# Hourglass attention and an ELU feed-forward on one core: attention rebuilt with four tokens per partition and DMA transposes

## The chip, the core and the metric

The kernel runs on one core of a Trainium2 chip. Its engines are TensorE (PE, matrix products from SBUF into PSUM), VectorE (DVE), ScalarE (ACT), GpSimd (POOL) and SyncE (SP, which here only issues transfers); 16 DMA engines serve them. The metric is the time of one execution on the device, in microseconds (us), on the slowest core; here there is one.

## What is computed

The inputs are q, k and v of shape (8 batches, 8 heads, 576 tokens, 64), float32, and the feed-forward's weights of 512 x 2048 and 2048 x 512. Two attentions are added, and the sum goes through the feed-forward:

```python
# per batch and head; sm_attn = softmax(scale * q k^T) v, softmax with the row maximum subtracted
out_up = np.repeat(sm_attn(mean4(q), mean4(k), mean4(v)), 4, axis=2)   # 144 pooled tokens
mask = np.abs(pos[:, None] - pos[None, :]) < 4                         # 7 neighbours
out_local = softmax(np.where(mask, scale * q @ k.T, -1e9)) @ v
x = (out_up + out_local)            # to 4608 tokens x 512
h = x @ w_in
out = np.where(h > 0, h, np.exp(np.minimum(h, 0)) - 1) @ w_out
```

`mean4` is the mean over four consecutive tokens. The feed-forward takes by far most of the arithmetic.

## The kernel before

Work is cut by batch b and by pair of heads j (four pairs of two heads; a pair fills the 128 partitions with 2 x 64 dimensions). `attn_p1(b, j, den)` loads q, k and v of a pair (rows of 256 bytes, issued by SP), turns q and k by float32 transposes on TensorE (L145, L148) into `qt` and `kt`, sums four tokens on GpSimd (L155, L158), and computes the scores with **keys on partitions** and queries along the free axis: 6 windows of 102 keys by 96 queries (L195) and two halves of the pooled attention (L177). ACT takes the exp without a row maximum (L183, L201); DVE multiplies the local scores by a mask of zeros and ones (L205). The denominators of all 8 heads of a batch, three rows a head, are gathered in one PSUM tile `den` by matmuls with indicator columns (L209, L215).

After the four pairs, `p1_group` takes the reciprocals of `den` (L313) and stores them to DRAM. `attn_p2` reads them back, broadcast over 128 partitions (`rcpb`, L227), multiplies the exps (L233), and multiplies by v (L238, L252); DVE adds the pooled part, each column repeated four times, into `XT` (L257), which holds all 4608 tokens.

The feed-forward runs in nine blocks of 512 tokens. `moe_mm1` makes 16 chunks of 128 hidden units (four matmuls each, L269), then exp on ACT (L274) and two operations on DVE (L276, L277) into `gt`, one buffer. `moe_mm2` makes four output tiles of 16 matmuls each (L287), copied by ACT and stored by SP. The program interleaves them: batch b's `p1` with block b-2's `mm1`, and `p2` of batch b-1 with the same block's `mm2`; three blocks run alone at the end. The weights are loaded on ACT's queue after batch 0's first part and cast by DVE. The framework's planner puts the instructions of each engine into a fixed order from this program order and places the waits; each engine and each queue then runs strictly in order.

## Time and profile before

Three runs: 543.38 us median (539.27 to 544.61). The profiled execution:

| | |
|---|---|
| span, first to last instruction | 543.6 us |
| PE busy | 471.4 us (87%) |
| DVE busy | 283.3 us (52%) |
| ACT busy | 240.5 us (44%) |
| POOL busy | 89.0 us (16%) |
| bytes moved by DMA | 59.53 MB, mean 110 GB/s |
| packets | 136219, of them 120240 under 512 bytes |
| mean granted TensorE clock | 0.953 of full speed |

An engine's busy time is the time in which it executed at least one instruction. A row of a group names the line, the engine, the operation, the tiles written and read, the shapes and the count, then the busy time in us and the mean of one in ns, then the idle time before it and what ended it. Matmuls overlap in the pipeline, so their mean is longer than what each adds to PE's time.

### The profile page before, as it was taken

How to read it: one execution, taken by the hardware profiler on the slowest of the kernel's cores; microseconds unless marked ns; L12 is line 12 of the kernel's file. 1: busy time of each engine (PE TensorE's matmuls, PEld its weight loads, DVE VectorE, ACT ScalarE, POOL GpSimd, SP SyncE). 2: the span in 40 equal slices, each digit the busy share in tenths (PEclk: the TensorE clock that was granted, in tenths of full speed). 3: DMA queues.
4: the chain of work that ended last, by engine and by line, in shares of the span. 5: the costliest groups of instructions: out<-in, count | busy, mean ns of one | idle time of the engine just before them, and what ended most of it. 6: DMA issues, size and time to landing. Idle time of an engine off the chain costs nothing.

```text
span 543.6 us, 8740 instructions
## 1 busy us (share of the span) xinstructions
PE 471.4 (87%) x2952; PEld 251.6 (46%) x2952; DVE 283.3 (52%) x627; ACT 240.5 (44%) x501; POOL 89.0 (16%) x260
## 2 busy tenths in 40 slices
PE   1538588788899998999999999999999877999997
PEld 0325355444444554545454545554545443444443
DVE  1212415733653665477456745774567677728180
ACT  1325463355533663367236723772367102535351
POOL 1113432212122122211122112211210000000000
PEclk9999999987898899989899989998989995999999
DMA  7776755534265435552464246524610340020202
GB/s 232 203 201 199 206 120 143 127 78 123 54 152 133 128 88 134 164 118 60 112 158 122 63 110 159 130 59 109 158 55 1 85 135 24 0 78 0 78 0 77
DMA packets 136219, 59.53 MB, mean 110 GB/s; under 512 B 120240, under 2 KB 129008, under 8 KB 135664
## 3 DMA queue, kind: packets, MB, share of 16 engines
q1 hardware_dynamic: 133488, 50.60, 37.4%
q10 hardware_dynamic: 2688, 8.39, 4.4%
q8 instruction: 23, 0.38, 0.3%
q14 instruction: 20, 0.16, 0.1%
HBM read 49.41 MB, written 9.55 MB: 108 GB/s over the span
## 4 chain that ended last, share of the span: by engine, by line
PE 70%; DMA 11%; DVE 6%; ACT 5%; SPq 4%; issue 2%; POOL 2%; ACTq 0%; POOLq 0%
PE hp L269 24%; PE op L287 24%; PE tp L145 6%; DMA kn<-in_k_dram 4%; PE den L209 3%; PE av L252 3%; PE sc L195 3%; ACT kt L149 2%; DMA w_491<-in_moe_w_out_dram 1%; DMA v_292<-in_v_dram 1%; PE vdp L165 1%; DMA rcpb<-rgd 1%; ACT qt L149 1%; PE davp L238 1%; PE den L215 1%
## 5 line engine op out<-in xcount | busy, mean ns | idle before, releaser
L287 PE MATMUL op<-WO,gt 128*128 128x512 f16 x576 | 132.3, 390 | 0.4 <-DVE gt L277 0.3
L274 ACT ACTIVATE e<-hp 128x512 f16<-128x512 f32 x144 | 85.9, 599 | 79.7 <-PE hp L269 78.1
L277 DVE SCALAR_TENSOR_TENSOR gt<-hp,ec 128x512 f16<-128x512 f32 x144 | 97.2, 686 | 3.2
L287 PEld LDWEIGHTS <-gt 128*128 128x128 f16 x576 | 57.6, 101 | 70.2 <-issue 7.6
L269 PEld LDWEIGHTS <-WI 128*128 128x128 f16 x576 | 55.4, 102 | 66.7 <-issue 10.3
L276 DVE TENSOR_SCALAR ec<-e 128x512 f16<-128x512 f16 x144 | 40.3, 287 | 59.6 <-ACT e L274 59.4
L292 ACT COPY os<-op 128x512 f32<-128x512 f32 x36 | 21.1, 585 | 112.4 <-PE op L287 105.2
L269 PE MATMUL hp<-XT_80,WI 128*128 128x512 f16 x144 | 59.1, 410 | 0.4 <-ACT aex L201 0.4
L205 DVE TENSOR_TENSOR mex<-aex,MASK 102x576 f16<-102x576 f16 x64 | 30.4, 478 | 54.5 <-ACT aex L201 52.3
L269 PE MATMUL hp<-XT_81,WI 128*128 128x512 f16 x144 | 57.7, 400 | 0.0
L269 PE MATMUL hp<-XT_83,WI 128*128 128x512 f16 x144 | 57.1, 397 | 0.0
L269 PE MATMUL hp<-XT_82,WI 128*128 128x512 f16 x144 | 57.1, 397 | 0.0
L243 DVE TENSOR_TENSOR outdt<-davp,rcpb 64x144 f16<-64x144 f32 x64 | 19.5, 304 | 59.8 <-PE davp L238 58.3
L145 PE MATMUL tp<-IDT,qn 128*128 128x128 f32 x128 | 33.2, 349 | 14.5 <-DMA qn<-in_q_dram 7.7
L145 PE MATMUL tp<-IDT,kn 128*128 128x128 f32 x128 | 33.9, 346 | 12.9 <-DMA kn<-in_k_dram 6.9
L201 ACT ACTIVATE aex<-sc 102x288 f16<-102x288 f32 x128 | 42.8, 416 | 4.1 <-PE sc L195 3.4
L252 PE MATMUL av<-anr,vw 102*64 102x96 f16 x384 | 35.2, 225 | 10.1 <-DVE anr L233 8.7
L233 DVE TENSOR_TENSOR anr<-mex,rcpb 102x576 f16<-102x576 f16 x64 | 29.3, 469 | 22.4 <-DMA rcpb<-rgd 21.7
L155 POOL TENSOR_TENSOR th<-kt 128x288 f16<-128x288 f16 x32 | 21.4, 670 | 84.6 <-ACT kt L149 84.5
L155 POOL TENSOR_TENSOR th<-qt 128x288 f16<-128x288 f16 x32 | 21.8, 680 | 82.4 <-ACT qt L149 82.4
L209 PE MATMUL den<-mex,INDC 102*24 102x288 f16 x128 | 32.4, 347 | 1.8 <-DVE mex L205 1.6
L252 PEld LDWEIGHTS <-vw 102*64 102x64 f16 x384 | 25.0, 120 | 18.7 <-issue 7.2
(140 smaller groups left out, 490.7 us busy)
## 6 DMA issues: line engine op xcount, KB each, us to landing
rcpb<-rgd SPq DMA_DIRECT2D x64, 180.0 KB
out_dram<-os SPq DMA_DIRECT2D x36, 256.0 KB
qn<-in_q_dram SPq DMA_DIRECT2D x64, 128.0 KB
kn<-in_k_dram SPq DMA_DIRECT2D x64, 128.0 KB
w32i<-in_moe_w_in_dram ACTq DMA_DIRECT2D x4, 1024.0 KB
w_482<-in_moe_w_out_dram ACTq DMA_DIRECT2D x1, 1024.0 KB
qn<-in_q_dram SPq DMA_DIRECT2D x64, 16.0 KB
w_485<-in_moe_w_out_dram ACTq DMA_DIRECT2D x1, 1024.0 KB
```

What stands on the lines that cost most here:

```text
L145: nc.tensor.transpose(tp[:, 128 * c : 128 * c + 128], srcn[:, c, :, :], IDT[:])
L155: nc.gpsimd.tensor_tensor(out=th[:, w_, :], in0=sl[:, 0 : S : 2], in1=sl[:, 1 : S : 2], op=AB.add)
L201: nc.scalar.activation(out=aex[0:KW, g, :], in_=sc[0:KW, 0:HHALF], func=AF.Exp, scale=SCALE)
L205: nc.vector.tensor_tensor(out=mex[0:KW], in0=aex[0:KW], in1=MASK[0:KW], op=AB.mult)
L209: nc.tensor.matmul(den[0:24, 0:HHALF], INDC[0:KW, rr + g, :], mex[0:KW, g, :], start=False, stop=False,)
L233: nc.vector.tensor_tensor(out=anr[0:KW], in0=mexs[hh][0:KW], in1=rcpb[0:KW, 0:S], op=AB.mult)
L252: nc.tensor.matmul(av[r0 : r0 + 64, co : co + QCH], vw[0:KW, c, hh, :], anr[0:KW, g, co : co + QCH], start=True, stop=True,)
L269: nc.tensor.matmul(hp[:, 0:TBLK], WI[:, dc, 128 * fc : 128 * fc + 128], XT[dc][:, t0 : t0 + TBLK], start=(dc == 0), stop=(dc == DMC - 1),)
L274: nc.scalar.activation(out=e[:], in_=hp[:, 0:TBLK], func=AF.Exp)
L276: nc.vector.tensor_scalar(out=ec[:], in0=e[:], scalar1=1.0, scalar2=-1.0, op0=AB.min, op1=AB.add)
L277: nc.vector.scalar_tensor_tensor(out=gt[:, fc, :], in0=hp[:, 0:TBLK], scalar=0.0, op0=AB.max, in1=ec[:], op1=AB.add,)
L287: nc.tensor.matmul(op_[:, 0:DM], gt[:, fc, 128 * t_ : 128 * t_ + 128], WO[:, fc, :], start=(fc == 0), stop=(fc == FCN - 1),)
```

## The change

Attention is written anew; the feed-forward's arithmetic stays as it was.

- **Layout.** Four consecutive tokens share a partition: `load_main` reads 128 of a batch's 144 groups of four for all eight heads in one transfer of 1 MB, in runs of 1 KB, and the 16 groups left over (tails) are loaded for two or four batches together. Batch 0's q and k are loaded by SP; nearly all else, the weights too, by POOL's queue, through three staging buffers.
- **Turning.** q, k and v are cast to fp16 for a whole batch (`cast_qk`), four tokens are summed by adds of contiguous rows (`pool_sum`), and q and k are transposed by the DMA engines (`dma_start_transpose` on SP, L178) instead of TensorE. `fill_q` puts q into token order (`Q2`).
- **Scores** (`a_unit`, one of eight per batch): **queries on partitions**, windows of 104 keys; the mask is added by a matmul of two small factors that puts -60000 into PSUM before the scores are accumulated. DVE takes the row maximum (L262, L267); ACT takes the exp with it as bias, one instruction per window. The exps are transposed by DMA (L289, L293).
- **Products** (`b_local`, `b_down`): v carries a column of ones, so the denominator comes out as a 65th column; `norm` adds 1e-9, takes the reciprocal and multiplies on DVE. The results are transposed by DMA (L343, L345), and POOL adds local and pooled parts into `XT`, now a ring of three blocks.
- **Order.** Batch 0's attention runs alone. Then 288 slots follow, 32 per block (16 of `mm1`, 16 of `mm2`, four matmuls each), and a table `plan` names the slots at which loads, casts and units of later batches stand. `XT` of batch b must be there by slot 32 b. PSUM is eight banks under one name.

The core of the diff; lines that repeat or only rename are left out:

```diff
-            tp = pt("tp", "tp2", 1024)
-            for c in range(4):
-                nc.tensor.transpose(
-                    tp[:, 128 * c : 128 * c + 128], srcn[:, c, :, :], IDT[:]
-                )
-            nc.tensor.transpose(tp[:, 512:576], srcn[0:64, 4, :, :], IDT[0:64, 0:64])
-            nc.scalar.copy(out=dst[:, off : off + S], in_=tp[:, 0:S])
...
-            nc.vector.tensor_tensor(out=mex[0:KW], in0=aex[0:KW], in1=MASK[0:KW], op=AB.mult)
-            mexs.append(mex)
-            rr = 3 * (2 * j + hh)
-            for g in range(2):
-                nc.tensor.matmul(
-                    den[0:24, 0:HHALF], INDC[0:KW, rr + g, :], mex[0:KW, g, :],
-                    start=False, stop=False,
-                )
-            for g in range(2):
-                last = (j, hh, g) == (3, 1, 1)
-                nc.tensor.matmul(
-                    den[0:24, 0:SD], INDC[0:72, rr + 2, :], dexs[hh][0:72, g, :],
-                    start=False, stop=last,
-                )
...
-            rcpb = sb.tile([128, S + SD], FP16, tag="rcpb", bufs=4, name="rcpb")
-            nc.sync.dma_start(
-                out=rcpb[:],
-                in_=bass.AP(tensor=rgd.tensor, offset=rgd.offset + h3 * HHALF,
-                            ap=[[0, 128], [1, S + SD]]),
-            )
-            anr = sb.tile([128, 2, HHALF], FP16, tag="anr", bufs=4, name="anr")
-            nc.vector.tensor_tensor(
-                out=anr[0:KW], in0=mexs[hh][0:KW], in1=rcpb[0:KW, 0:S], op=AB.mult
-            )
...
-                nc.vector.tensor_tensor(
-                    out=xc, in0=av[r0 : r0 + 64, 0:HHALF],
-                    in1=_rep4(outdt[r0 : r0 + 64, 72 * g : 72 * g + 72]), op=AB.add,
-                )
...
+    def load_main(name, b, eng=None):
+        t = staging(name).rearrange("p (h x) -> p h x", h=H)
+        s = srcs[name][b].rearrange("h (a r) d -> a h (r d)", r=4)
+        (eng or nc.gpsimd).dma_start(out=t, in_=s[0:128])
+        stage[name, b] = t
...
+    nat = {}
+
+    def cast_qk(name, b, eng, pool=None):
+        t = stage.pop((name, b))
+        n = sb.tile([128, 5, 512], FP16, tag="nat", bufs=2, name="nat_" + name)
+        cast(qk_view(n), t, 0, 128, SCALE if name == "q" else 1.0, eng)
+        pool_sum(n[:, 4, :], n, 0, 128, 512, pool)
+        nat[name, b] = n
...
+    def turn_qk(name, b):
+        n = nat.pop((name, b))
+        dst = QT if name == "q" else KT
+        nc.sync.dma_start_transpose(
+            out=dst[:].rearrange("p s j a -> p (s j) a")[:, :, 0:128],
+            in_=n[:].rearrange("p s f -> p (s f)"),
+        )
+
+    def fill_k(b, eng):
+        eng.tensor_copy(
+            out=KT[:].rearrange("p s j a -> p (s j) a")[:, :, 128:NQ],
+            in_=KTT[:].rearrange("p s j a -> p (s j) a")[:, :, 16 * b : 16 * b + 16],
+        )
+
+    def fill_q(b, eng, big):
+        eng.tensor_copy(out=QT[:, 4, :, 128:NQ], in_=QTT[:, 4, :, 16 * b : 16 * b + 16])
+        for src, a0, a1, o in ((QTT, 128, NQ, 16 * b - 128), (QT, 0, 128, 0)):
+            big(
+                out=Q2[:, :, 4 * a0 : 4 * a1].rearrange("p j (a r) -> p j r a", r=4),
+                in_=src[:, 0:4, :, a0 + o : a1 + o].rearrange("p r j a -> p j r a"),
+            )
...
+        for c in range(NC6):
+            w = _win(c)
+            n0 = max(0, min(CW, 128 - w))
+            put(0, c, V16, w, n0)
+            if n0 < CW:
+                put(4 * n0, c, V16T, 16 * b, CW - n0)
+        nc.sync.dma_start(out=VDT[0:16, :], in_=VDA[16 * b : 16 * b + 16, :])
...
+    def a_unit(b, j, g):
+        if g == 0:
+            i = serial["a"] % 2
+            serial["a"] += 1
+            cur["P"] = (PL[i], PD[i])
+        pl, pd = cur["P"]
+        bk = [bank("sc"), bank("sc")]
+        for hh in range(2):
+            nc.tensor.matmul(
+                bk[hh][0:NL, 0 : 3 * NK], MU[64 * hh : 64 * hh + 36, :],
+                MV[64 * hh : 64 * hh + 36, g, :], start=True, stop=False,
+                skip_group_check=True,
+            )
+        for cc in range(3):
+            c = 3 * g + cc
+            w = _win(c)
+            for hh in range(2):
+                r0 = 64 * hh
+                nc.tensor.matmul(
+                    bk[hh][0:NL, NK * cc : NK * cc + NK],
+                    Q2[r0 : r0 + 64, j, NL * c : NL * c + NL],
+                    KT[r0 : r0 + 64, 0:4, j, w : w + CW],
+                    start=False, stop=True, skip_group_check=True,
+                )
+        for hh in range(2):
+            r0 = 64 * hh
+            nc.tensor.matmul(
+                bk[hh][0:QH, 3 * NK : 3 * NK + NQ],
+                QT[r0 : r0 + 64, 4, j, QH * g : QH * g + QH],
+                KT[r0 : r0 + 64, 4, j, :], start=True, stop=True,
+                skip_group_check=True,
+            )
+        mx = sb.tile([128, 2, 4], FP32, tag="mx", bufs=4, name="mx")
+        md = sb.tile([128, 2], FP32, tag="md", bufs=4, name="md")
+        for hh in range(2):
+            nc.vector.tensor_reduce(
+                out=mx[0:NL, hh, 0:3],
+                in_=bk[hh][0:NL, 0 : 3 * NK].rearrange("p (c x) -> p c x", c=3),
+                axis=AX.X, op=AB.max, negate=True,
+            )
+            nc.vector.tensor_reduce(
+                out=mx[0:QH, hh, 3:4], in_=bk[hh][0:QH, 3 * NK : 3 * NK + NQ],
+                axis=AX.X, op=AB.max, negate=True,
+            )
+        nc.vector.tensor_scalar(
+            out=md[0:QH, :], in0=mx[0:QH, :, 3], scalar1=0.0625, scalar2=None, op0=AB.mult
+        )
+        for hh in range(2):
+            for cc in range(3):
+                nc.scalar.activation(
+                    out=pl[:, 3 * g + cc, hh, 0:NK].rearrange("p (a r) -> p r a", r=4),
+                    in_=bk[hh][0:NL, NK * cc : NK * cc + NK].rearrange(
+                        "p (r a) -> p r a", r=4
+                    ),
+                    func=AF.Exp, bias=mx[0:NL, hh, cc : cc + 1], scale=1.0,
+                )
+            nc.scalar.activation(
+                out=pd[0:QH, g, hh, 0:NQ], in_=bk[hh][0:QH, 3 * NK : 3 * NK + NQ],
+                func=AF.Exp, bias=md[0:QH, hh : hh + 1], scale=0.0625,
+            )
+        if g == 1:
+            pt = sb.tile([128, 2 * NC6, NL], FP16, tag="pt", bufs=5, name="pt")
+            nc.sync.dma_start_transpose(
+                out=pt[:], in_=pl[:].rearrange("p c h k -> p (c h k)")
+            )
+            pdt = sb.tile([128, 8, 80], FP16, tag="pdt", bufs=5, name="pdt")
+            nc.sync.dma_start_transpose(
+                out=pdt[:], in_=pd[:].rearrange("p g h k -> p (g h k)")
+            )
+            turned[b, j] = (pt, pdt)
...
+    def b_local(b, j, hh):
+        pt, pdt = turned[b, j]
+        if hh == 0:
+            i = serial["b"] % 2
+            serial["b"] += 1
+            cur["X"] = (XL[i], XD[i])
+        xl, xd = cur["X"]
+        bk = bank("av")
+        h = 2 * j + hh
+        for c in range(NC6):
+            nc.tensor.matmul(
+                bk[0:NL, VH * c : VH * c + VH], pt[0:NK, 2 * c + hh, :],
+                VW[:, c, VH * h : VH * h + VH], start=True, stop=True,
+                skip_group_check=True,
+            )
+        norm(bk, NL, NC6, xl[:, :, hh, :])
+
+    def norm(bk, n, m, dst):
+        o = bk[0:n, 0 : m * VH].rearrange("p (c x) -> p c x", x=VH)
+        dn = sb.tile([128, NC6, 1], FP32, tag="dn", bufs=4, name="dn")
+        nc.vector.tensor_scalar(
+            out=dn[0:n, 0:m], in0=o[:, :, D:VH], scalar1=1e-9, scalar2=None, op0=AB.add
+        )
+        rc = sb.tile([128, NC6, 1], FP32, tag="rc", bufs=4, name="rc")
+        nc.vector.reciprocal(out=rc[0:n, 0:m], in_=dn[0:n, 0:m])
+        nc.vector.tensor_tensor(
+            out=dst, in0=o[:, :, 0:D], in1=rc[0:n, 0:m].to_broadcast([n, m, D]), op=AB.mult
+        )
+
+    def b_down(b, j):
+        pt, pdt = turned.pop((b, j))
+        xl, xd = cur["X"]
+        bk = bank("avd")
+        for g in range(2):
+            for hh in range(2):
+                h = 2 * j + hh
+                i = 2 * g + hh
+                for kc, vd in ((0, VD), (1, VDT)):
+                    nc.tensor.matmul(
+                        bk[0:QH, VH * i : VH * i + VH], pdt[:, 2 * i + kc, 0:QH],
+                        vd[:, VH * h : VH * h + VH], start=(kc == 0), stop=(kc == 1),
+                        skip_group_check=True,
+                    )
+        norm(bk, QH, 4, xd[0:QH].rearrange("p g h d -> p (g h) d"))
+        xlt = sb.tile([128, NC6, NL], FP16, tag="xlt", bufs=2, name="xlt")
+        nc.sync.dma_start_transpose(out=xlt[:], in_=xl[:].rearrange("p c h d -> p (c h d)"))
+        xdt = sb.tile([128, 2, 80], FP16, tag="xdt", bufs=2, name="xdt")
+        nc.sync.dma_start_transpose(out=xdt[:], in_=xd[:].rearrange("p g h d -> p (g h d)"))
+        for g in range(2):
+            for c0, c1 in pieces(b, g):
+                n = c1 - c0
+                pos = (S * b + NL * c0) % RING
+                cc = c0 - 3 * g
+                nc.gpsimd.tensor_tensor(
+                    out=XT[:, j, pos : pos + NL * n].rearrange("p (a r) -> p a r", r=4),
+                    in0=xlt[:, c0:c1, :].rearrange("p c (a r) -> p (c a) r", r=4),
+                    in1=xdt[:, g, CH * cc : CH * (cc + n)]
+                    .rearrange("p (a o) -> p a o", o=1)
+                    .to_broadcast([128, CH * n, 4]),
+                    op=AB.add,
+                )
...
+    def mm1(m, fc):
+        if fc == 0:
+            gt_of[m] = sb.tile([128, FCN, TBLK], FP16, tag="gt", bufs=1, name="gt")
+        gt = gt_of[m]
+        pos = (TBLK * m) % RING
+        hp = bank("hp")
+        for dc in range(DMC):
+            nc.tensor.matmul(
+                hp[:], WI[:, dc, 128 * fc : 128 * fc + 128],
+                XT[:, dc, pos : pos + TBLK], start=(dc == 0), stop=(dc == DMC - 1),
+            )
+        e = sb.tile([128, TBLK], FP16, tag="e", bufs=3, name="e")
+        nc.scalar.activation(out=e[:], in_=hp[:], func=AF.Exp)
+        ec = sb.tile([128, TBLK], FP16, tag="ec", bufs=2, name="ec")
+        nc.vector.tensor_scalar(
+            out=ec[:], in0=e[:], scalar1=1.0, scalar2=-1.0, op0=AB.min, op1=AB.add
+        )
+        nc.vector.scalar_tensor_tensor(
+            out=gt[:, fc, :], in0=hp[:], scalar=0.0, op0=AB.max, in1=ec[:], op1=AB.add
+        )
...
+    load_tails("q", 0, nc.sync)
+    load_tails("k", 0, nc.sync)
+    load_main("q", 0, nc.sync)
+    load_main("k", 0, nc.sync)
+    load_tails("v", 0, nc.sync)
...
+    fill_k(0, V)
+    fill_q(0, V, A.copy)
+    prep_v(0, "dve", V)
+    load_w("o", 0, G)
+    spread_v(0)
+    a_unit(0, 0, 0)
+    cast_w("i", 0, "dve")
...
+    b_down(0, 3)
+    cast_qk("k", 1, "dve", V)
+    turn_qk("k", 1)
+    fill_k(1, V)
+    fill_q(1, V, A.copy)
+    load_main("v", 1)
...
+    AS = (0, 1, 3, 5, 7, 9, 11, 13)
+    BS = (0, 2, 4, 6)
+    for b in range(1, B):
+        end = 32 * b
+        if b > 1:
+            c0 = {2: 15, 3: 42, 4: 69}.get(b, end - 64)
+            at({2: 11, 3: 33}.get(b, end - 70), load_main, "q", b)
+            at({2: 12, 3: 33}.get(b, end - 70), load_main, "k", b)
+            at(end - 38, load_main, "v", b)
+            at(c0, cast_qk, "q", b, "act", V)
+            at(c0 + 1, turn_qk, "q", b)
+            at(c0 + 3, cast_qk, "k", b, "act", V)
+            at(c0 + 4, turn_qk, "k", b)
+            at(c0 + 10, fill_k, b, G)
+            at(c0 + 11, fill_q, b, G, A.copy)
+            at(end - 30, prep_v, b, "act", V)
+            at(end - 22, spread_v, b)
+        for u in range(8):
+            s0 = {1: 0, 2: 27, 3: 54}.get(b, end - 47) + 2 * u
+            at(s0, a_unit, b, u // 2, u % 2)
+        for j in range(4):
+            at(end - 16 + BS[j], b_local, b, j, 0)
+            at(end - 16 + BS[j], b_local, b, j, 1)
+            at(end - 15 + BS[j], b_down, b, j)
+
+    for m in range(NTOK // TBLK):
+        for i in range(32):
+            if i < 16:
+                mm1(m, i)
+            else:
+                mm2(m, i - 16)
+            for fn, args in plan.pop(32 * m + i, []):
+                fn(*args)
+    assert not plan, plan
```

## The prediction

> **What bounds the kernel now.** I read the page's shares first, then the slices, then the chain of waits in order of time, then the groups split by shape, last the DMA queues. The shares and two rows of slices (each digit a fortieth of the span, 13.6 us):
>
> ```profile
> span 543.6 us, 8740 instructions
> ...
> PE 471.4 (87%) x2952; PEld 251.6 (46%) x2952; DVE 283.3 (52%) x627; ACT 240.5 (44%) x501; POOL 89.0 (16%) x260
> ...
> PE   1538588788899998999999999999999877999997
> ...
> DMA  7776755534265435552464246524610340020202
> ```
>
> TensorE is the bound from slice 9 on, but not before: in the first eight slices DMA is at 5 to 7 tenths and PE only climbs. No other engine comes near its span. The chain of waits (start, duration, what) gives the rhythm: each pair of `op` runs is one 512-token block of the feed-forward.
>
> ```profile
> 111.18 2.65 PE hp L269 x11
> ...
> 208.67 6.91 PE op L287 x32
> ...
> 371.01 8.59 PE op L287 x32
> ...
> 484.66 13.81 PE hp L269 x64
> 498.48 13.81 PE op L287 x64
> 512.29 13.81 PE hp L269 x64
> 526.10 13.83 PE op L287 x64
> ```
>
> From 208.67 to 371.01 three periods pass: 54.1 us each. In that stretch PE is busy 51.6 us per period (busy time by stretch, 154.75 for three). A block with nothing beside it takes 27.6 us (two runs of 64 matmuls, 13.81 each), so attention costs PE 24.0 us per period for 224 small matmuls, 107 ns each. The span divides into: ramp to the first `hp` at 107 us; six periods with attention, to 437; the second half of the last batch's attention alone, to 454; three blocks alone, to 540; last copy and store 3.6. DMA bounds the ramp, PE the rest. The span (543.6) and the median of the runs (543.38) agree, so I sum against the span.
>
> **Prices from the trace** (line, engine, operation, shapes, count; busy, mean ns):
>
> ```profile
> L277 DVE SCALAR_TENSOR_TENSOR gt<-hp,ec 128x512 f16<-128x512 f32 x144 | 97.2, 686 | 3.2
> L276 DVE TENSOR_SCALAR ec<-e 128x512 f16<-128x512 f16 x144 | 40.3, 287 | 59.6 <-ACT e L274 59.4
> L205 DVE TENSOR_TENSOR mex<-aex,MASK 102x576 f16<-102x576 f16 x64 | 30.4, 478 | 54.5 <-ACT aex L201 52.3
> L243 DVE TENSOR_TENSOR outdt<-davp,rcpb 64x144 f16<-64x144 f32 x64 | 19.5, 304 | 59.8 <-PE davp L238 58.3
> ...
> L292 ACT COPY os<-op 128x512 f32<-128x512 f32 x36 | 21.1, 585 | 112.4 <-PE op L287 105.2
> L201 ACT ACTIVATE aex<-sc 102x288 f16<-102x288 f32 x128 | 42.8, 416 | 4.1 <-PE sc L195 3.4
> ```
>
> DVE from PSUM: 144 columns 304 ns, 512 columns 686, so about 1.04 ns a column on 155 ns. DVE adds from SBUF: 478 ns for 576, 0.83 a column. ACT: `e` with 512 columns takes 599, `aex` with 288 takes 416: 0.82 ns a column on 181.
>
> **The change, part by part, per batch of eight heads.**
>
> PE. Gone: 224 matmuls, among them the float32 transposes. New: 160 (ten per half of a head pair, L235 to L253; twelve and eight per pair, L308, L336). At the 107 ns of today's mix: 17 us, beside 27.6 for a block: 44.7. In the same stretch the cheapest comparable row (the `sc` matmuls, 11.58 us for 144, 80 ns) gives 13, the dearest (`den`, 10.10 for 48, 210 ns) 34. I take 17; the long mask product of 312 columns is only 16 of the 160.
>
> DVE. Feed-forward 16 x (0.287 + 0.686) = 15.6. Row maxima, not in the trace: a unit has two of 312 columns and two of 144, by the line 2 x (480 + 305) = 1.57, plus one tiny scale at 0.155: 1.7; eight units 13.8. Normalizing 384 and 256 columns, each with two tiny operations: 8 x 0.90 + 4 x 0.75 = 10.2. Sums of four tokens (1024 and 512 columns at 0.83): 1.27 each for q, k, v: 3.8. Tails, spread: 2. Gone: 19 us of masks, normalizers, output adds and reciprocals. Sum **45 us**: DVE goes from 32 busy of 54 to a second bound. If a reduction costs half the line, 38; if twice, 58.
>
> ACT. 48 exps of 104 columns at 0.266, 16 of 144 at 0.299: 17.6; 18 `e` at 0.6: 10.8; three casts and one copy of 2048 columns, 1.86 each: 7.4; 4.5 `os` at 0.585: 2.6. Sum 38. Row sums come with the ones column, so nothing is added for them.
>
> POOL: nine XT adds at the 0.68 of its `th` row (288 columns), 6 us, and the input loads, which leave SP for POOL. POOL issues none before; the nearest rows are `w_482` at 450 ns and `os` at 357 on other queues. Even ten times that, for five loads a batch, is 20 us of a free engine. But XT adds queue behind loads that wait for a staging buffer; I charge nothing, and keep 3 us a block for the range.
>
> How the three sum: the program puts score units and value products into the sixteen `mm2` slots of a block, and one `gt` buffer keeps the halves apart. First half: DVE bounds, 15.6 plus sums and tails, 20 us against PE 13.8. Second half: PE bounds, 13.8 + 17 = 30.8, against DVE 24, ACT 20. With a little leak between halves: **50 us** a block. Complete mixing gives 45, DVE's sum; no leak and 150 ns per small matmul give 58.
>
> DMA transposes, all on SP. Per batch 4 x (295 + 164 + 147 + 41 KB) + 2 x 655 KB = **3.9 MB**. No row of the trace shows one; the queues bound it:
>
> ```profile
> q1 hardware_dynamic: 133488, 50.60, 37.4%
> q10 hardware_dynamic: 2688, 8.39, 4.4%
> ```
>
> Columns: packets, MB, share of 16 engines' span. q10: 142 ns per 3.1 KB packet, 351 GB/s on 16 engines; q1: 24.4 ns per packet, 379 bytes on average, most of them rows of 256 bytes. So 3.9 MB costs 11 us as long rows, 23 as 256-byte rows, 93 if packets carry 64 bytes at the same 24.4 ns. I take 23, the nearest row (128 fp16 elements are 256 bytes). Other traffic, interpolated between the two packet prices: loads in 1 KB rows 11, stores 3.5, V windows 2. DMA is then at 40 of 50 us: close, but under the block.
>
> The Trainium skill has two rules here. "DMA: Bandwidth & Descriptors", section "Latency and other measured facts", gives 261 GB/s measured for a DMA transpose: 15 us a batch, an estimate, and the sum stays as it is. "VectorE: DVE Perf Modes", section "The three transpose paths", speaks against the change: 1309 ns for 128 x 128 by DMA against 390 on TensorE. This trace's PE transposes have 346 to 349 ns. If 152 such blocks a batch ran one after another that would be 199 us a batch and some 1,520 in all, an estimate. No run so far shows which holds.
>
> On SP a transpose waits for ACT's last exp of the pair, and behind it stand output stores and the transposes of finished products; only XT's readers, PE at the block's start, feel that. Score units run some 16 slots ahead of their use, 25 us at 50 a block, which covers 4 us transposes; without that cover each late XT is a gap on PE.
>
> Ramp. Before the first score: 2.9 MB at the first slice's 232 GB/s, 14 us with start-up; k's cast (a 2048-column cast is 1.23 on DVE), sums, both transposes at 4 us plus 2: 28 us. Then DVE has eight units (13.8), normalizing (10.2), five weight casts (6.3), next q and k (3.8): 34 us. The last pair's way through transposes, products, transposes and adds: 8. **70 us**, against 107 for a batch and a half today. Ends: 55 if DVE's work overlaps loading, 100 if the weight loads, chained through three staging buffers, set the pace.
>
> Sum: 70 + 7 x 50 + two blocks alone (DVE 15.6 + PE 13.8 each, 59) + 3 = **482 us**. Gained: 37 in the ramp, 17 from the lone attention at 437, some 8 in the loop.
>
> **Rivals.**
> - Mixing is complete, ramp 58: 58 + 315 + 59 + 3 = 435. For it: PE and ACT run several slots apart through eight PSUM banks; against: one `gt`. Chance 0.14.
> - SP's order makes XT late: 6 us more a block, 524. For it: 18 transposes, 8 V copies and 4 to 5 stores a batch share SP's one in-order queue, and a store waiting for its `os` holds what is behind it (SP's waits today: 118.2 us for `os` in 32 waits, the longest 26.2). Chance 0.16.
> - Slower: the crossing itself bounds. Place: SP's queue and the 16 DMA engines in every block. Break-even is (543.6 - 132) / 7 = 58.8 us a block, less 17 for other traffic: 41.8 us for 3.9 MB, 93 GB/s, or 142 bytes a packet at 24.4 ns. At 64 bytes a block is 110 us and the kernel 902; at 110 bytes, 54 + 17 = 71, so 629. For it: only packets price small transfers in this trace; against: 256-byte source rows. Chance 0.20, all on the other side.
> - The change doesn't do what it says, the loop still PE-bound at today's 54 with today's ramp: 107 + 378 + 62 = 547; chance 0.02.
>
> **Numbers.** The forecast has 0.48 (455 to 515). Faster by over 1%: 0.78; within 1%, about what a measurement tells from no change: 0.02; slower: 0.20. The range leaves out the lower half of the 435 case and the dear half of the slower one: 435 to 585.
>
> **What would show it.** Right: first `hp` near 70 us; periods of 50; DVE busy near 45 a period and the largest releaser of PE; transposes landing in 3 to 6 us. Wrong: PE waiting on `pt`, `xlt` or `QT` by DMA, long SP waits, DMA share above 9 tenths in the loop, or a reduction far from 480 ns.

## The result, and the profile after

The changed kernel takes **581.4 us** (median; 576.74 to 585.1), against 542.08 for the one before: 1.073 times as long, 95% interval 1.067 to 1.080. The forecast was 482 us and faster; the measured time lies inside the stated range only because the range had room for the slower cases: a gain was forecast, and a loss came. The profiled execution has a span of 579.3 us. Where some runs of a kernel lie over 1.5% above its fastest, the times below are the medians of its other runs.

The page of the changed kernel: shares, then the slices of PE and DMA (one digit is 14.5 us), then the queues (packets, MB, share of 16 engines).

```profile
span 579.3 us, 7874 instructions
...
PE 374.1 (65%) x2432; PEld 185.9 (32%) x2432; DVE 326.8 (56%) x982; ACT 312.7 (54%) x732; POOL 97.0 (17%) x147
...
PE   0001244087544887615976689878968987989997
...
DMA  9897789979898796599759787776559256040101
...
q1 hardware_dynamic: 145880, 50.18, 49.5%
q0 software_dynamic: 8512, 33.82, 21.0%
```

PE has 97 us less work than before, and nothing else is a bound over the whole span. What has changed is where DMA stands: at 7 to 9 tenths in nearly every slice up to the middle, and just there PE is low. A share over the span hides this. Cut at the first `op` matmul of each block (142.2, 215.6, ... us) it shows. The columns are the stretch, its length, the busy time of PE, weight loads, DVE, ACT and POOL, then the granted clock, DMA share and GB/s:

```profile
0.00:95.60 95.60, 13.85 (x160) 11.60 (x161) 37.12 (x99) 29.36 (x71) 16.83 (x28) 1.00 0.92 192
95.60:142.20 46.60, 26.04 (x149) 10.98 (x148) 30.33 (x74) 27.11 (x65) 12.91 (x15) 0.96 0.96 153
142.20:215.60 73.40, 47.50 (x289) 22.85 (x288) 41.09 (x126) 42.08 (x105) 14.26 (x23) 0.81 0.87 163
215.60:290.30 74.70, 46.02 (x289) 22.11 (x288) 42.24 (x125) 42.67 (x92) 15.91 (x24) 0.77 0.84 189
290.30:349.00 58.70, 42.60 (x290) 21.31 (x289) 34.49 (x113) 41.47 (x91) 9.28 (x13) 0.88 0.78 157
349.00:399.70 50.70, 41.70 (x290) 20.97 (x289) 34.24 (x115) 36.81 (x90) 9.82 (x13) 0.90 0.76 174
399.70:450.60 50.90, 41.96 (x290) 20.64 (x289) 34.40 (x115) 36.80 (x90) 7.47 (x15) 0.87 0.68 132
450.60:500.20 49.60, 41.82 (x290) 20.86 (x289) 34.32 (x117) 29.71 (x89) 5.28 (x8) 0.86 0.41 88
```

The last three periods take 50.4 us on average: the forecast's 50. The first three take 73.4, 74.7 and 58.7 with the same 289 or 290 matmuls, and the first `op` comes at 142.2 us where the forecast had 90 (ramp 70, then 20 for a first half). So the 97 us between forecast and span are: **52 before the first `op`, 58 in the six periods (57 of them in the first three), and 13 less** from there to the end, because the seventh interval (33.6 us) carries only the products of the last batch and was charged with its scores too.

What was waited for in the changed kernel (engine, line, releaser; us in total, times, longest):

```profile
POOL XT L351 <- DMA xdt<-XD: 223.4, 28, 33.3
PEld L245 <- ACT Q L192: 76.4, 4, 47.0
ACT Q L192 <- DMA QT<-nat_q: 71.0, 4, 29.1
ACT PL L276 <- DMA pt<-PL: 34.0, 5, 9.6
DVE XL L323 <- DMA xlt<-XL: 32.4, 7, 14.1
```

POOL is idle anyway, so its 223.4 us cost nothing by themselves. The other four are the chain of attention: PE waits for ACT's copy, ACT's copy waits for the transpose of q, and ACT and DVE wait until a transpose has read the buffer that they are to fill. Near its beginning the chain that ended last (start, duration) has the longest piece of the whole execution:

```profile
20.64 27.59 DMA QT<-nat_q
48.26 4.73 ACT Q L192
```

The forecast had 6 us for it.

### The profile page after: what moved, and what is told of

Its sections match the earlier page's. It is cut to its first block, busy times and chain, and to the rows that moved or that the text cites. A ratio compares the mean times of both kernels' runs of the same rounds, so it can differ in the third digit from the quotient of the medians.

```text
span 579.3 us, 7874 instructions
## 1 busy us (share of the span) xinstructions
PE 374.1 (65%) x2432; PEld 185.9 (32%) x2432; DVE 326.8 (56%) x982; ACT 312.7 (54%) x732; POOL 97.0 (17%) x147
## 3 DMA queue, kind: packets, MB, share of 16 engines
q1 hardware_dynamic: 145880, 50.18, 49.5%
## 4 chain that ended last, share of the span: by engine, by line
DMA 30%; PE 26%; DVE 16%; ACT 12%; issue 7%; SPq 6%; POOL 1%; ACTq 0%; DVEq 0%; POOLq 0%
PE op L421 11%; PE hp L398 11%; DMA pt<-PL 8%; ACT PL L276 6%; DMA xlt<-XL 6%; DMA QT<-nat_q 5%; DMA xdt<-XD 4%; DVE gt L408 3%; DMA KT<-nat_k 3%; DVE ec L405 3%; ACT e L403 3%; DMA st_v<-in_v_dram 3%; DVE mx L262 2%; DMA pdt<-PD 2%; DVE XL L323 2%
## 5 line engine op out<-in xcount | busy, mean ns | idle before, releaser
L398 PE MATMUL hp<-XT,WI 128*128 128x512 f16 x576 | 153.7, 425 | 36.6 <-POOL XT L351 16.7
L276 ACT ACTIVATE PL<-sc,mx 96x104 f16<-96x104 f32 x384 | 123.2, 511 | 78.3 <-DVE mx L267 35.8
L262 DVE TENSOR_REDUCE mx<-sc 96x3 f32<-96x312 f32 x128 | 59.9, 468 | 68.3 <-PE sc L253 63.6
L351 POOL TENSOR_TENSOR XT<-xlt,xdt 128x288 f16<-128x288 f16 (+2 forms) x72 | 47.8, 687 | 223.4 <-DMA xdt<-XD 223.4
L245 PE MATMUL sc<-KT,Q 64*96 64x104 f16 x384 | 28.9, 236 | 83.6 <-ACT Q L192 60.0
L192 ACT COPY Q<-QT 128x2048 f16<-128x2048 f16 x8 | 38.3, 4792 | 71.0 <-DMA QT<-nat_q 71.0
L323 DVE TENSOR_TENSOR XL<-av,rc 96x384 f16<-96x384 f32 x64 | 35.2, 551 | 32.4 <-DMA xlt<-XL 32.4
L283 ACT ACTIVATE PD<-sc,md 72x144 f16<-72x144 f32 x128 | 50.4, 405 | 2.9 <-DVE md L271 2.7
L235 PE MATMUL sc<-MV,MU 36*96 36x312 f16 x128 | 29.7, 364 | 23.6 <-ACT PD L283 11.1
L308 PEld LDWEIGHTS <-pt 104*96 104x96 f16 x384 | 27.1, 141 | 51.6 <-DMA pt<-PL 26.6
L267 DVE TENSOR_REDUCE mx<-sc 72x1 f32<-72x144 f32 x128 | 37.7, 294 | 0.1
```

The source lines that it names most:

```text
L245: nc.tensor.matmul(bk[hh][0:NL, NK * cc : NK * cc + NK], Q2[r0 : r0 + 64, j, NL * c : NL * c + NL], KT[r0 : r0 + 64, 0:4, j, w : w + CW], ...
L262: nc.vector.tensor_reduce(out=mx[0:NL, hh, 0:3], in_=bk[hh][0:NL, 0 : 3 * NK].rearrange("p (c x) -> p c x", c=3), axis=AX.X, op=AB.max, ne ...
L276: nc.scalar.activation(out=pl[:, 3 * g + cc, hh, 0:NK].rearrange("p (a r) -> p r a", r=4), in_=bk[hh][0:NL, NK * cc : NK * cc + NK].rearrange(
L283: nc.scalar.activation(out=pd[0:QH, g, hh, 0:NQ], in_=bk[hh][0:QH, 3 * NK : 3 * NK + NQ], func=AF.Exp, bias=md[0:QH, hh : hh + 1], scale=0 ...
L308: nc.tensor.matmul(bk[0:NL, VH * c : VH * c + VH], pt[0:NK, 2 * c + hh, :], VW[:, c, VH * h : VH * h + VH], start=True, stop=True, skip_gr ...
L323: nc.vector.tensor_tensor(out=dst, in0=o[:, :, 0:D], in1=rc[0:n, 0:m].to_broadcast([n, m, D]), op=AB.mult)
```

## The experiments

**The theory after the result:** the crossing alone is cheap enough, but a transpose that is under way while 1 MB loads are under way too is stretched several times, and the new kernel asks for both at once in its first half. **Rivals:** SP's in-order queue, where transposes stand behind output stores that wait for `os`; the two score and product buffers, which come free only with a transpose; compute (PE's lower clock, ACT's dearer exps); the volume of the transposes as such.

The following table has all runs with the starts of the `op` halves, taken from the trace of one execution each, so that a gain can be placed. "Periods" are the distances between them. For `e9_qk_pe` that execution took 561.4 us.

| run | median us | against before | first `op` | next six periods |
|---|---|---|---|---|
| changed | 581.4 | 1.073 | 142.2 | 73.4, 74.7, 58.7, 50.7, 50.9, 49.6 |
| e1_store_act | 595.8 | 1.103 | 140.0 | 80.5, 84.6, 59.0, 50.3, 49.2, 47.5 |
| e2_four_x | 576.9 | 1.065 | 133.7 | 77.6, 70.5, 60.7, 53.0, 51.2, 46.7 |
| e3_no_loads | 525.0 | 0.971 | 121.4 | 60.6, 55.6, 52.9, 51.1, 50.8, 49.6 |
| e4_no_exp_turn | 537.4 | 0.992 | 124.9 | 67.7, 74.4, 53.4, 47.9, 44.7, 43.1 |
| e5_late_w | 568.0 | 1.045 | 128.6 | 65.4, 80.2, 60.2, 50.4, 51.0, 49.6 |
| e6_load_act | 581.9 | 1.071 | 142.8 | 51.6, 97.5, 53.8, 55.9, 53.5, 46.8 |
| e7_load_sp | 569.7 | 1.048 | 150.6 | 59.0, 69.5, 57.4, 50.4, 50.9, 48.4 |
| e8_q2_runs | 571.7 | 1.052 | 129.4 | 73.2, 85.9, 49.9, 50.9, 48.1, 47.8 |
| e9_qk_pe | 551.9 | 1.017 | 113.1 | 88.2, 58.7, 53.5, 60.9, 54.4, 51.4 |
| e10_pe_b0 | 522.3 | 0.963 | 105.0 | 74.7, 54.8, 51.3, 56.9, 49.1, 48.3 |
| e11_pe_b01 | 523.6 | 0.965 | 117.2 | 61.1, 60.4, 50.1, 57.6, 48.3, 48.0 |
| e12_pe_all | 580.0 | 1.068 | 118.5 | 66.5, 68.1, 61.0, 63.8, 63.3, 56.9 |
| e13_more_buffers | 562.0 | 1.036 | 135.6 | 70.6, 66.1, 60.1, 50.9, 52.4, 43.7 |
| e14_no_tails | 558.9 | 1.030 | 148.4 | 64.0, 57.6, 59.3, 51.3, 49.9, 48.5 |
| e15_best | 483.7 | 0.895 | 106.5 | 73.3, 48.8, 42.8, 45.4, 43.5, 42.0 |

### Loads left out, transposes left out

```diff
     def load_main(name, b, eng=None):
-        t = staging(name).rearrange("p (h x) -> p h x", h=H)
+        if b > 0:
+            stage[name, b] = held[name]
+            return
+        t = keep("held_" + name, [128, DFF], FP32)[:].rearrange("p (h x) -> p h x", h=H)
+        held[name] = t
```

> The loads of q, k and v of batches 1 to 7 (22 MB of the 84.7) are left out: those batches use batch 0's, which stay in SBUF, and staging for weights and tails has two buffers in place of three. If the transposes are slow because loads share their DMA engines, a transpose lands near its undisturbed time (the later blocks show 4 us for the exps) and the blocks fall from 58 to near 50 us: 520 to 540. If the crossing is slow by itself or DVE and PE set the blocks, above 565.

Measured 525.0 us (0.971 of before, 0.963 to 0.979), 56 less than the changed kernel. This is what the theory expects, and the places are the ones it needs: 21 us less before the first `op`, 13, 19 and 6 in the first three periods, and nothing in the last three. In the trace the same stretches are shorter with the same matmuls on PE:

```profile
121.40:182.00 60.60, 43.25 (x289) 20.21 (x288) 39.40 (x126) 41.15 (x103) 10.92 (x20) 0.87 0.85 133
182.00:237.60 55.60, 41.84 (x289) 20.59 (x289) 38.98 (x123) 38.89 (x93) 7.14 (x14) 0.88 0.67 130
237.60:290.50 52.90, 41.24 (x289) 20.90 (x288) 32.95 (x111) 40.49 (x90) 6.03 (x10) 0.90 0.59 115
```

The transposes themselves show it too. These are the longest of the chain that ended last in the first three periods (start, duration from issue to landing), of the changed kernel first:

```profile
153.99 10.04 DMA pt<-PL
174.97 8.62 DMA KT<-nat_k
248.56 10.01 DMA KT<-nat_k
299.78 12.37 DMA xlt<-XL
```

And without the loads:

```profile
128.32 5.17 DMA pt<-PL
139.91 7.86 DMA KT<-nat_k
160.14 8.34 DMA pt<-PL
189.49 4.92 DMA KT<-nat_k
```

In all, the transposes of q, k, exps and products are 62 us of that chain in these three periods, and 34 without the loads: 28 of the 38 us that the periods gain. Leaving the loads out also takes out the waits for the loads themselves (`st_v`, 3% of the changed kernel's chain), so not all of the 56 us belong to the transposes.

Next the transposes of the exps:

```diff
-            nc.sync.dma_start_transpose(
-                out=pt[:], in_=pl[:].rearrange("p c h k -> p (c h k)")
-            )
...
-            turned[b, j] = (pt, pdt)
+            turned[b, j] = (PT0, PDT0)
```

> The transposes of the exps are left out (14.7 MB, 64 of 150 transposes); the products use a constant tile in their place, so they don't wait for the scores either. If volume and waits of the transposes bound the loop, it falls by 6 to 10 us a block and the ramp by some 15: 490 to 525. If compute bounds it (PE with its clock at 0.8 to 0.9, or ACT's exps at 511 ns where 266 were worked out), 555 or more.

Measured 537.4 us (0.992 of before, 0.987 to 0.997), 44 less than the changed kernel but 12 more than the upper end of what the theory expected, and under the 555 or more that was expected if compute bounds the kernel. But the run leaves a wait out as well as 14.7 MB, so it can't tell volume from latency. It does price the crossing, as an average that holds the stretched packets too. SP's queue in this run, columns as above:

```profile
q1 hardware_dynamic: 86488, 35.49, 35.0%
```

49.5% of 579.3 us is 286.8 us of 16 engines; 35.0% of 535.6 is 187.5. The 99.3 us between them moved 14.7 MB: **148 GB/s**, with 59,392 packets fewer (256 bytes a packet and a few small ones). A batch's 3.9 MB so costs 26.3 us, where 23 were taken.

### The order on SP, the buffers, the tails

```diff
-            nc.sync.dma_start(out=out[r0 : r0 + 128, :], in_=os_[:])
+            nc.scalar.dma_start(out=out[r0 : r0 + 128, :], in_=os_[:])
```

> The 36 output stores go to ACT's queue, everything else as in the changed kernel (581.4 us). If SP's order is what costs the loop (its queue waits 108.5 us for os, and transposes stand behind), those waits leave SP and the loop shortens by several us a block: 545 to 565. If transposes are late because of what the DMA engines carry, or because buffers come free late, the same transposes are as late as before: 575 to 585.

Measured 595.8 us (1.103, 1.095 to 1.112): **slower by 14 us**, which neither theory had. SP's 108.5 us of waits for `os` are gone and nothing is gained, which speaks against the rival that SP's stores hold up the transposes; why the first two periods grow by 7 and 10 us isn't shown, and what the issues cost ACT wasn't separated.

```diff
-    XL = [keep(f"XL{i}", [NL, NC6, 2, D]) for i in range(2)]
+    XL = [keep(f"XL{i}", [NL, NC6, 2, D]) for i in range(4)]
```

> Four buffers XL and XD in place of two, so that normalizing the next pair needn't wait until the transpose has read the pair before last. If the two buffers cost (DVE waits 32.4 us for xlt's transposes and stands with feed-forward work behind it), 545 to 565. If the end of a block is set by when the last transposes land, DVE merely runs ahead and XT comes as late: 570 to 583.

Measured 576.9 us (1.065, 1.058 to 1.072): 4.5 us less, the second theory's range. With the score buffers too:

```diff
-    PL = [keep(f"PL{i}", [NL, NC6, 2, 128]) for i in range(2)]
+    PL = [keep(f"PL{i}", [NL, NC6, 2, 128]) for i in range(3)]
```

> Three PL and PD and four XL and XD in place of two each, else the changed kernel. ACT waited 34.0 us for PL's transposes, DVE 32.4 for XL's; four XL alone gave 577. If those waits hold the early blocks, 555 to 568. If they only hand on that the DMA engines are late, 572 to 578.

Measured 562.0 us (1.036, 1.029 to 1.043): 19 us less. ACT's wait for `pt` and DVE's wait for `xlt` are gone from the largest waits; what is left there of `pt` is PE's wait for the data. So the buffers, which come free only when a stretched transpose has landed, carry a part of the loss to ACT and DVE. Their gain lies before the first `op` (7 us), in the first (3), second (9) and sixth period (6); the third to fifth change by less than 2.

```diff
-    for t_, s0 in ((1, 2), (2, 34)):
+    for t_, s0 in ():
```

> The tails of batches 2 to 7 (16 of 144 groups of each) are left out, with their loads, casts, sums and four of the six tail transposes; constants stand in their place. They fall into blocks 0 and 1: some 7 us of DVE and 4 of ACT in each, 2.4 MB of loads. If that work is why those blocks are slow, they fall from 73 and 75 to 60 to 65: 555 to 565. If the 1 MB loads and the crossings alone do it, 575 or more.

Measured 558.9 us (1.030, 1.021 to 1.040): 22 us less, in the expected range. The periods of blocks 0 and 1 fall from 73.4 and 74.7 to 64.0 and 57.6, while the first `op` comes 6 us later. The tails' work on DVE and ACT, their loads and four of their transposes are gone together, so this run doesn't say which of them counts; it says that the two slow blocks are slow by what is put into them.

### Which loads, which queue

```diff
+        if late:
+            nc.vector.tensor_copy(out=t[0:1, 0:1], in_=KT[0:1, 4, 3, 0:1])
```

> The first weight loads start only when K of batch 0 has been transposed (a one-element copy from K into each staging buffer makes them wait), and the order of the later weight, q and k loads is moved back accordingly. If loads in flight stretch the transposes, Q and K of batch 0 land some 10 to 15 us after issue in place of 27.6, the first score comes near 40 us in place of 53, and the kernel takes 565 to 573. If the weights then arrive late for the first block, or the transposes are as slow without loads, 580 or more.

Measured 568.0 us (1.045, 1.039 to 1.051), as expected. This run has the theory in one view. From its timeline (start, duration, engine or queue, line, what; SP's rows last as long as SP is held):

```profile
20.87 4.04 SPq L178 DMA_TRANSPOSE QT<-nat_q  x1
25.00 3.13 SPq L178 DMA_TRANSPOSE KT<-nat_k  x1
...
26.47 4.72 ACT L192 COPY Q<-QT 128x2048 f16<-128x2048 f16 x1 [7.03 <-DMA QT<-nat_q]
...
30.37 1.63 POOL L373 DMA_DIRECT2D st_w<-in_moe_w_in_dram  x3 [11.22 <-DVE st_w L371]
...
44.34 16.49 SPq L289 DMA_TRANSPOSE pt<-PL  x1
```

And the changed kernel's SP for the same step:

```profile
20.64 15.99 SPq L178 DMA_TRANSPOSE QT<-nat_q  x1
36.73 11.66 SPq L178 DMA_TRANSPOSE KT<-nat_k  x1
```

Without weights under way, q lands 5.6 us after its issue (20.87 to 26.47) in place of 27.6, and holds SP 4.0 us in place of 16.0: the same transpose, the same 655 KB. It isn't alone even so. By the trace's packet records nearly all of v's load of 1 MB goes out beside it in both kernels (219 and 224 packets of 4 KB); what only the changed kernel has beside q's transpose are 512 packets of 8 KB, the first four weight loads. So the weights stretch it; whether by their volume (4.2 MB) or by their large packets no run separates. But once POOL has issued the weights (30.37), a transpose of exps, half as large, holds SP for 16.49 us. In that time the DMA engines moved 121 GB/s, against 285 in q's 5.6 us, so more than a full pipe is at work. The cost has mostly moved, which is why 22 us of earlier scores brought 13 in all.

```diff
-        (eng or nc.gpsimd).dma_start(out=t, in_=s[0:128])
+        (eng or nc.scalar).dma_start(out=t, in_=s[0:128])
```

> The 1 MB loads of q, k and v go to ACT's hardware queue in place of POOL's. On SP's queue such rows went out as packets of 1 KB (53 ns), on POOL's as packets of 4 KB (159 ns). If the DMA engines alternate between queues packet by packet, transposes get a larger share beside a load: 555 to 572. If only the volume on the DMA engines counts, 577 to 590, the upper end if ACT, which runs in order, stands at staging buffers.

Measured 581.9 us (1.071, 1.063 to 1.078): no change in all, though the first period is 22 us shorter and the second 23 longer. By the trace's packet records these loads now went out in packets of 1 KB (median 46 ns). So smaller packets of q, k and v brought nothing here; the weights and tails kept their 8 KB and 4 KB, and smaller packets there weren't tried.

> The same loads go to SP's queue, in one queue with the transposes: no alternation, but whatever is behind a load waits for all of it (some 4 us), and for its staging buffer. If alternation between queues is the cost, 560 to 575. If SP's order is what counts, or the volume, 585 to 610.

Here `nc.sync` stands in the same line. Measured 569.7 us (1.048, 1.042 to 1.052): 12 us less, and none of the harm that SP's order was to do. One queue for loads and transposes is better than two in this kernel. Q's transpose of the ramp still took 32.3 us there, beside the weights, which stayed on POOL. Whether the gain comes from transposes and loads no longer being mixed, or from other instants of issue, is open.

### What compute costs

```diff
-        for src, a0, a1, o in ((QTT, 128, NQ, 16 * b - 128), (QT, 0, 128, 0)):
-            big(
-                out=Q2[:, :, 4 * a0 : 4 * a1].rearrange("p j (a r) -> p j r a", r=4),
-                in_=src[:, 0:4, :, a0 + o : a1 + o].rearrange("p r j a -> p j r a"),
-            )
+        for j in range(4):
+            big(
+                out=Q2[:, j, :].rearrange("p (c r a) -> p r c a", c=NC6, r=4),
+                in_=QT[:, 0:4, j, :].rearrange("p r (c a) -> p r c a", c=NC6),
+            )
```

> q is copied with the 24 groups of a window contiguous (runs of 48 bytes) in place of single elements 8 bytes apart; the mask factor and POOL's add take the new order of rows. The copy took 4.8 us on ACT where 1.86 was worked out, and the first score waits for it. If that sum is right for contiguous runs, it falls to 2 to 3 us, and the kernel by 3 us in the ramp and 1 to 2 us in each early block: 568 to 576. If ACT has slack there, 578 to 583.

Measured 571.7 us (1.052, 1.041 to 1.062), the middle of two runs at 568.2 and 575.1, in the expected range; two more lie at 577.6 and 582.5, so that a gain of this size is not sure. The copy itself: 4 x 671 ns for 576 columns each, 2.7 us, against

```profile
L192 ACT COPY Q<-QT 128x2048 f16<-128x2048 f16 x8 | 38.3, 4792 | 71.0 <-DMA QT<-nat_q 71.0
```

Writing single fp16 elements 8 bytes apart made a column twice as dear as in runs of 48 bytes (2.34 ns against 1.16), and the copy 2.6 times the 1.86 us that the forecast took from other rows.

### TensorE for the transposes

```diff
-        nc.sync.dma_start_transpose(
-            out=dst[:].rearrange("p s j a -> p (s j) a")[:, :, 0:128],
-            in_=n[:].rearrange("p s f -> p (s f)"),
-        )
+        for i0, i1 in ((0, 8), (8, 16), (16, 20)):
+            tq = ps.tile([128, 8, 128], FP16, tag="bank", bufs=8, name="tq")
+            for i in range(i0, i1):
+                nc.tensor.transpose(tq[:, i - i0, :], n[:, i // 4, 128 * (i % 4) : 128 * (i % 4) + 128], IDT[:])
+            nc.scalar.copy(out=d[:, i0:i1, 0:128], in_=tq[:, 0 : i1 - i0, :])
```

> q and k are transposed by TensorE (40 matmuls a batch with an fp16 identity, copied from PSUM by ACT, 5 us a batch), as in the kernel before; the exps and the products stay with the DMA engines. If transposes beside loads are the cost: the 27.6 us for Q in the ramp goes, as do some 10 us of q and k in each early block: 540 to 555. If the volume of the remaining transposes keeps the early blocks slow, 565 or more; late blocks at 51 us or 2 to 4 more (PE 4, ACT 5).

Measured 551.9 us (1.017, 1.014 to 1.020): 29 us less, in the expected range. The gain lies before the first `op`, which comes 29 us earlier; the first period is 15 us longer.

> As the run before, and batch 0's exps and products by TensorE too, so that the ramp has no DMA transpose but the tails; with four XL buffers and q copied in runs. If loads and transposes hinder each other only while weights and first batches are loaded, the first feed-forward matmul comes at 55 to 65 us in place of 95.6, and the kernel takes 505 to 525, below the one before. If compute sets the ramp, 535 to 550.

Measured 522.3 us (0.963, 0.958 to 0.969), **faster than both kernels**. The first feed-forward matmul comes at 68.7 us, 4 later than expected at the upper end; the second period falls to 54.8.

> As the run before, with batch 1 by TensorE too. Block 0 (73 us from its output matmuls to the next block's) is the one in which batch 1 goes all the way; without DMA transposes, and 15 us more on PE and 10 on ACT and DVE, it should take 60: 495 to 520. If PE's added work takes what the DMA gives, equal to the run before.

Measured 523.6 us (0.965, 0.960 to 0.969): the same as the run before. Block 0 falls from 74.7 to 61.1, but the first `op` comes 12 us later: the added work is merely placed elsewhere.

> All transposes but the tails by TensorE, for all batches. Late blocks: PE 27.6 + 17 + 15 = 60 us in place of 51, so 7 x 60 + 65 + 59 + 3 = 547 if PE bounds them. If it comes out below the two runs before, DMA transposes are worth nothing even in the late blocks.

Measured 580.0 us (1.068, 1.065 to 1.070), 33 more than the sum expected. The late periods, 60 by that sum, are near it; the first `op` comes only at 118.5 us, and the first two periods take 66.5 and 68.1 with hardly any DMA transposes. So the beginning is slow in part for another reason than the crossing. The late periods are 61.0 to 63.8 us where the changed kernel has 51, with 52.8 us of PE busy per period in place of 41.8, and DMA nearly idle:

```profile
314.10:377.90 63.80, 53.35 (x442) 29.55 (x441) 38.59 (x123) 45.62 (x110) 10.21 (x13) 0.84 0.25 77
```

So DMA transposes are no mistake as such. In the late blocks they are worth 11 us each against the changed kernel; in the ramp, where PE is idle and the loads come, they cost.

> q and k turned by TensorE, batch 0 wholly so, q copied in runs, three PL and PD, four XL and XD, and the 1 MB loads on SP's queue. If buffers and alternation add what they gave alone, 505 to 517, else 520 to 526 as without them.

Measured **483.7 us** (0.895 of before, 0.887 to 0.903), far below what was expected, and 17% below the changed kernel. Its page:

```profile
PE 376.7 (78%) x2864; PEld 206.0 (43%) x2864; DVE 333.0 (69%) x990; ACT 332.9 (69%) x808; POOL 87.4 (18%) x129
...
PE 54%; ACT 13%; DMA 13%; DVE 12%; issue 4%; POOL 1%; SPq 1%; ACTq 0%; DVEq 0%; POOLq 0%
```

PE is again the bulk of the chain that ended last (54%, against 26% in the changed kernel, where DMA had 30%). The late periods fall to 42 to 45 us, which none of the parts gave alone but for one sixth period (43.7 with more buffers). Which of them together do it wasn't tried, so this gain is not explained; block 0 still takes 73.3.

## Why the prediction was wrong

1. **The ramp, 70 us.** "Both transposes at 4 us plus 2" is the step that failed first. The first score was to come at 28 us and came at 53.0, because q's transpose took 27.6 us in place of 6 while four weight loads were under way; without them it took 5.6. From the first score to the first `hp` (95.6) it is then 42.6 us where 42 were worked out. The forecast put the loads of the ramp one after the other ahead of the transposes, and never asked what POOL's queue issues while SP transposes. Its own other end, "100 if the weight loads set the pace", came nearer, by another way: not the weights were late, but the transposes beside them.

   Another 27 us lie in the first half of block 0, which took 46.6 us (95.6 to 142.2) where 20 were charged. The forecast put score units into the second halves; the plan puts all eight of batch 1 into slots 0 to 14, and in this half PE has 80 matmuls of `sc`, DVE is busy 30.3 us and ACT 27.1. With the loads left out it still took 42.0, and with hardly any DMA transposes, but their work on PE, 48.5. So most of these 27 us come from the work that stands there, a part of which the forecast charged later.

2. **"DMA is then at 40 of 50 us: close, but under the block."** The price was fair: 26.3 us for the transposes of a batch where 23 were taken from the 256-byte packets (148 GB/s). What failed is the inference from the mean. Attention goes through the DMA engines four times in turn (load, q and k, exps, products), each step waits for the one before, and plan and tails put the loads of several batches into the first three blocks. There the DMA share is 0.78 to 0.87, and the periods took 58.7 to 74.7 us; with the loads out, 52.9 to 60.6. "Covers 4 us transposes" held in the late blocks, where those of the exps on the chain took 3.9 to 4.1, and not with 7 to 12.

3. **"50 us a block"** was right for the last three periods (50.4), but not by its terms, so the agreement is partly luck. PE was busy 41.8 (forecast 44.7) and ACT 30 to 37 (38). DVE was busy 34.3, not 45: the rows' means were summed, but consecutive DVE instructions overlap in the records (row maxima of 0.47 us start 0.39 before the next), so the busy time of a stretch would have been the better price. The single term was good: 468 and 294 ns for the row maxima, where 480 and 305 were worked out.

4. **ACT's terms.** An exp with bias took 511 ns by its mean, 321 by busy time over count, where 0.266 us was taken; the q copy 4.8 in place of 1.9. ACT was not the bound, so the first cost little; the second stood on the path of the ramp.

5. **The slower rival** had the right sign and the wrong mechanism. It needed less than 93 GB/s everywhere; measured were 148, and the late periods, with a DMA share of 0.41 to 0.76, show that the crossing isn't the bound there, though they were 3 to 7 us shorter still without the exps' transposes. "SP's order makes XT late" was tried by itself, and the stores on another queue brought no gain.

6. Two rules of the Trainium skill were weighed. "DMA: Bandwidth & Descriptors", section "Latency and other measured facts", has 261 GB/s; 148 were measured here, an average that holds the packets stretched by loads. "VectorE: DVE Perf Modes", section "The three transpose paths", has 1309 ns for a 128 x 128 block by DMA and 390 on TensorE. 152 blocks a batch in 26.3 us are 173 ns each, an estimate from the run without exps' transposes, so 1309 ns is no price for a stream of them; 199 us a batch would also be 1,592 in all, not 1,520. The order of the two was right in the ramp, where PE is idle, and wrong in the late blocks, which took 11 us more with all transposes on TensorE.

## What to carry to other kernels

Price a transfer by what else is in flight when it starts, not by its volume over the whole span: list for each stretch what every queue issues, and give a transpose on the critical chain its short time only where little else runs beside it (5.6 us beside v's 1 MB, 27.6 beside four weight loads too). Work that is cheap on the DMA engines in the steady part can belong on an idle engine during the ramp; batch 0 and every batch's q and k on TensorE, q copied in runs, spare buffers for what a transpose must read, and one queue for loads and transposes together turned a loss of 7% into a gain of 10%. And look at where a plan puts the work of the first block, not only at how much it is.

## What the runs showed of the hardware

- **A stretched transpose keeps the engines busy.** By the trace's packet records a 256-byte packet took 27.6 ns on average in the changed kernel, where nearly all of them are transposes, at a median of 18; in the kernel before, where 112,512 are rows of loads, it took 18.0 on average. Between 36 and 48 us, with 128 packets of 8 KB beside them, 1,629 such packets took 111 ns on average at a median of 18: a few wait long, and DMA counts as busy meanwhile. How a crossing and a load hold each other up isn't shown by these runs.
- **The granted clock went with PE's gaps in most stretches, not in all.** It was 0.96 to 0.98 in three periods of the steady part before (PE busy 95% of the time), 0.81 and 0.77 in the slow blocks (65 and 62%), 0.86 to 0.90 in the late blocks (82 to 84%) and 0.96 in the late blocks of the fastest version (88 to 94%); but it was 1.00 in the changed kernel's ramp, with PE busy 14%. PE took 47.5 and 46.0 us in the two slow blocks for the number of matmuls that took 41.7 to 42.0 in the late ones. A part of what waits cost may so be paid a second time on PE; it wasn't measured by itself.
- A transfer issued by POOL held it for some 0.9 us in most of the 1 MB loads of q, k and v and 0.53 in most of the tails, where the rows of ACT's queue in the kernel before, 0.34 to 0.45, were the nearest known.
